# Attention with sparse heads and a gated MoE block: first five pairs' q and k in 2 KB runs, heads paired h and h+4, queries in natural order, one store a tile, one PSUM tensor, replanned

## The chip, the cores and the metric

The kernel runs on one core of one Trainium2 chip. The metric is device microseconds of one execution, as a median over runs. The profile is of one execution, with its own span (first to last instruction of the trace). The engines are TensorE (PE, its weight loads PEld), VectorE (DVE), ScalarE (ACT), GpSimd (POOL) and SyncE (SP), which issues nearly all the DMAs.

## What is computed

Four batches, eight heads, 768 positions, 64 dimensions a head, in float32. Heads 0, 2 and 6 are plain causal attention. The other five see only the first 4 keys and the last 64 (causally). The outputs of all heads are put side by side into x, 3072 tokens of 512, and go through a gated block with d_ff = 1536.

```python
scores = np.matmul(q, k.transpose(0, 1, 3, 2)) / np.sqrt(64)
causal = rel >= 0                              # rel = query position - key position
stream_keep = causal & (is_sink | (rel < 64))  # is_sink: key position < 4
mask = causal for heads 0, 2, 6, stream_keep for the others
a = softmax(where(mask, scores, -1e9))
x = a @ v, heads side by side                  # 3072 x 512
g = x @ w_gate
out = ((g * sigmoid(g)) * (x @ w_val)) @ w_out
```

## The kernel before

All matmuls are in float16 with float32 sums. The attention goes by tiles of 128 queries: 24 tiles, t = 0 to 23, in the order of TILES. Two tiles make a pair n of 256 positions of a batch (QP); a pair is the unit in which q, k and v are loaded.

Loads (`load`, L322): SP brings q, k or v of one pair into a `raw` buffer, 512 KB, as `h (p j) d -> p h (j d)` with j = 2. Partition p holds two neighbouring positions of every head, and each run in memory is 2 x 64 floats, 512 bytes. The even and odd positions of a 128-tile are therefore kept apart everywhere behind it ("j n" order: all even positions, then all odd ones). Weights come in blocks of 512 KB, in 1 KB runs (w_gate, w_val, L330) and 2 KB runs (w_out, L327). Blocks of w_gate and w_val are pieces of 256 columns.

Casts (`cast`, `castv`, `wcast`): ACT, DVE or POOL turns raw into float16 (lines L190, L192 and L196 are the helpers that issue them). q and k go to `hq`, v to `vt`, weights to `wg_sb`, `wv_sb` and `wo_sb`.

Transposes of q and k: for pairs 0 to 4 by TensorE (`transposes`, L420, eight of 128 x 128 to one PSUM bank `tr`), followed by copies to `qT` and `kT` on ACT or DVE (`evac`); for the later pairs by DMA (`dmat`, L409, on SP's queue). The two heads of one entry of PAIRS lie on the two halves of the partitions, [(0, 2), (4, 6), (1, 3), (5, 7)].

Scores (`scores`, L499): a unit is up to eight 128 x 128 blocks of scores in two PSUM banks (`sc`). A block is one matmul with 64 rows (one head); two of them, on the two row halves, can run side by side. For tiles 0 to 3 the masks are added in PSUM by matmuls of the constants `nat` with the identity. Then comes exp on ACT (L507, to `e`); in the later tiles a mask multiplies e (L516, DVE or POOL). `sinks_k` and `sinks_v` copy the first keys and values into place for the sparse heads. The value matmuls (L526) write `av`, DVE divides by the sums (L533, L534) into `xb`, and `xtranspose` turns it into `xt`, by TensorE for tiles 0 to 7 (L550) and by DMA afterwards (L544).

MoE: six groups of four tiles. Per group and per 128 columns of d_ff: four matmuls for the gate and four for the values (L687, 512 columns each, 256 in the first four steps of group 0), tanh on ACT (L693), two DVE steps (L697, L704) to `h`. Then the output product (L722), its copy to `o_sb` (`oevac`), and the stores (`store`, L743): two for a tile, since the rows of even and of odd positions lie on different partitions. The last tile's output is cut into 384 and 128 columns; there the second store of each piece goes out on ACT's queue.

Order: nothing is scheduled at run time. Each step is a task. ORDER, a string of task numbers that was planned beforehand, gives the order in which all tasks are issued, and so the order on each engine; WAYS says which engine does a task, SLOTS which buffer it uses. Numbers from FILL on are filler matmuls (`warm`, L300) on the identity, whose result is not used: 10 at the start and 11 later, all of them ahead of the first gate matmul. PSUM is split by pools: three banks for `gv` (gate, values, transposes), one for `o`, two buffers of two banks for `big` (scores, av). A task that takes a buffer waits for those that used it last.

Of the kernel before, what the change touches and what calls it, by code (L numbers as in the profile page):

```python
# [16 lines left out]
    "0306070200041I1J1Q1S1R01051K1Lxm1T1U1Vxi1W1X1f1g0A1q1r1z20211d1k1e081N1P1Mxj1Y1Z1a091o1p1w1y0C1O"  # L17
    "1h1i1j2K2Q2R1x2B2C292A2G0D2L2S2T0B1u1t0h22232U2V0g1b1c1m1n0n1s242526138q8r8s8g8h8i1v2D2E2F0y8M8N"
    "8O27280z8W8X2X2Y2f2a2b0m2I2J0F148j8k8Y8t8u8v8w8x0i8y8z8R8S8T2m2j2k2u118Z8a2Z0G2n0o108P8Q8U8V2l8b"
    "8c8d0E2H2y3435169091929596970l2W2p2q0k0I0r2z36370j17939498992M8e8f2N2O0H8l8m8n381l2c2d392e2P1F9U"  # L20
    "9V9W9Z9a9b8o8p2o3B3C3D0J3G3H1C9K9L3e3k3l2g2r2s2v2t0p0q3L3S3T9M0M1G9c9d303V3W199A9B9C3E3F333A3P9X"
    "9Y2h2w2x2i313I3Q3J3M3K3R3f3m3n9P9Q9R1A9D9E3u3v3U3X3Y9F9G9H3N3O323Z3a3b1D9S9T9N9O3r3s0s3o3z3p3c3d"
    "0T9I9JArAsAt0LAmAnAoAcAdAe0t15AfAg0u18ApAq9y9zA0AXAYAZAaAb4243444546470K3h4H4P4O0wAh3g4G4M4NA8A9"
    "AA129eA1A23q3w3t3x403yAuAv0x1HABAC0v1B4D4W4X4T4U4V0Q4w4z4x0N4K4L4IANAOAk9f4JAPAiAjAl0X4Y4Z0P3i48"
    "49A6ASATAU0eA3A4A5A70R1E9g9h9iAL4v52534Q6d3j4A4R4S4B4E4C0O0S9j9k9l9m9n4d4o4p4g4h4iAVAW414F4a4b4c"
    "4f4e0UAIAJAKAQAR4j4k4l4m4n9o9p9q4u514q4rADAE9r9t9u9v9w4yAG505E4s5455564t5O5V0W0c7A0YAFBkAHBlBLBM"
    "AwBmBOBNBPBnBo9x5WAM5N5U5T5B5C6k5D9sBpBqBrBfBgBhC9CACBCCCDC4C5C60VBT5758595A7j7rAxAy5z65AzB05R61"
    "785F5G5K5X5Y5Z5a5i5b5cBiBj606866B1B2B3B45d5e5r5s6eBsBt5H5I5L5J5M6364BuBvBwBzC05l5m5o5p5q5wC162B6"
    "B7B8B9BxBy5QBQBRBSBUBBBC5P5f5g5h5jBVBWBXC2C30Z6f6h6g6i676C6D6E696A5S0bBYBZ6lC7C85n5t5u5v5xBaBbBc"
    "BGBHBIBJBKBdBeBD6H6I5k6F6G6j5yDMDNDOCnCoCpD7D8D9DPDQ6B6J6K6L6NCxCyCzD0D1777E7FBABE6M6S6T6U6X6YCY"  # L30
    "DADB6m6x6n6y6o6pDCDDDEDHDIDJ6u736v6wCZ6O6P6Q6RCECFCGCqCrCaDKDLB5CHCJCKCL6z0dDUDFDGBFCMCO0f7l7kD2"
    "D3D40a6q6r6s7i70717274DRDSDTDVCPCQ767D7C7G7J7K7H7L7ICNCbCc6tCg6V6W7o7p7BCRCSCdCeCiCjCk6Z6a6b6cCI"
    "CTCUCfChCsCtCuCvCw7R7X7U7f7Y7Z7V7WCVCWD57a7b7nD67M7N79ClCm75E0E1E2EAEBECE3E4DqDrDsDtDuEFEGEHEIEJ"
    "EjEkElE5E6E7DvDwE8E9DxEZEa7O7P7Q7SDyDzEbEmEn7q7s7v7w7x7t7uDWDXDYDZDa80817yEeEfEg7c7d7g7e7zDbDcDd"
    "858B8C8D88898AEKELEcEdEN7T7h82838684DeDgDhDi8E8FEMEO8G8HDfEDEPEQER7m8I8J8K8LESETEhEiDjDlDmDnEEEU"
    "EVEWEXEY87FhFiFjFwFxFyFLF8F9FBCXDoDpEoEpEqFAFCFDFIFJErEtEsEuFKFMFNFOFPFQFRFEFFEvFkFlFGFHFmFnFoFc"
    "FdFeFXFYFfFgFZFuEwEyEzExF0F1F2DkFzFrFsF3F4G0FtFvG1G2G3FaFbFSFTFUF5F6F7FVFWFpFqG4G5G6G7G8G9GAGBGC"
    "GDGEGFGGGHGIGLGJGMGNGQGOGKGPGRGS"
)
WAYS = (  # L40
    "000000000000000000000000000000000000000000000000000000000000222222202202212222220200122001100100"
    "000000000000010022112212000011000000100000000000220021010100000100000210000000100000020022122000"
    "000010000000000100100000100000000022100201000010010000022000000000000220222222000000000000000002"
    "100010010000000012222200000010000000000000220012022000000000000000200001000000002202002010000001"
    "000000000010000000000000000120122000000000000000010002002222220000001000000001100000000000001002"
    "222000000000010000000000001001000000000000000000000000000000000000000000000000000000000000000000"
    "000000000000000000000000000000100001000000000000000000000000000000000000000000000000000000000000"
    "000000000100001000010000000000000000000000000000000000000000000000000000000000000000000000000000"
    "000000000000000000000000000000000000000000000000000000000000000000000000010000000000000010000000"
    "000000000000000000000000000000000000000000000000000000000100000000000000100000000000000000000000"  # L50
    "0000000000000000000000000000000000000000000000100000000000010"
)
SLOTS = (
    "0013427562C075931CADB91402567AB9387CD98D834BA1AB6D4285601010010000211011320215122041300240120012"
    "010121051403120120010110402000100513021113401100411020021304001012001511110402101302420100105141"
    "110100213020514011040021015030100511020411310012131200341300140211105020102100311041005120011021"
    "020321020111210100111021222002110002122410015011281112B1020A000291001701126000100012111F1100J012"
    "1H0121M000210011L2021K0021E2010C2101I1121D0000G01000101211091120N10128011261021A1110300110002140"
    "01051121B1100720002000101012010L1112C0000I0111M0011D0101H0122G1020J1002E012012002F2001K000000011"
    "102811120111060012N20217001190012A011222010B001142100521013010101011112C1010D2010I2110L2011E0110"  # L60
    "12011G1102M1100F0022J2021H1122K001100110"
# [57 lines left out]
def kernel(  # L119
# [45 lines left out]
    PAIRS = [(0, 2), (4, 6), (1, 3), (5, 7)]  # L165

    RINGS = {"raw": 14, "hq": 5, "e": 6, "xb": 3, "xt": 2, "sig": 2, "sil": 3,
             "h": 2 * NJ, "osb": 2, "gv": 3, "o": 1, "big": 2}
# [9 lines left out]
    for r in ("gv", "o", "big"):  # L178
        pools[r] = ctx.enter_context(tc.tile_pool(name="ps_" + r, bufs=1, space=PSUM))
# [3 lines left out]
    def buf(ring, shape, dt, name):  # L183
        return pools[ring].tile(shape, dt, name=name, tag=ring + running[-1].slots[ring])
# [50 lines left out]
    def keep(n, base, qstep, kstep):  # L235
        for j in range(2):
            part = nat[odds(j), n]
            nc.gpsimd.affine_select(
                out=part, in_=part, compare_op=ALU.is_ge, fill=OFF, base=base + kstep * j,
                pattern=[[0, n.stop - n.start], [qstep, 2], [2 * qstep, 64]],  # L240
                channel_multiplier=2 * kstep)
# [25 lines left out]
    def mask_fills(x):  # L267
        def run():
            for dst, src in FILLS[x]:
# [3 lines left out]
    FILLS = [[(m0[:, 0:3], BAND0), (m0[:, 3:4], DIAG), (m0[:, 4:6], BAND0), (m0[:, 6:8], DIAG),  # L273
              (m2[:, 2:5], DIAG), (m2[:, 1:2], OWN), (m1[:, 0:2], OWN)],
             [(m2[:, 0:1], FAR), (m1[:, 2:4], FAR)]]
# [37 lines left out]

    landed = {}

    def load(kind, n):
        r = buf("raw", [128, 1024], FP, "raw")
        landed[kind, n] = r
        if kind in "qkx":
            b, pi = QP[n]  # L320
            sl = slice(pi * 256, (pi + 1) * 256)
            nc.sync.dma_start(  # L322
# [52 lines left out]
    XQ = 5  # L375
    XK = 5

# [4 lines left out]
    def cast(n, kd, x):  # L382

        if (n, kd) not in hqs:
            hqs[n, kd] = buf("hq", [128, 1024], FH, "hq").rearrange(
                "p (k a x) -> p k a x", k=2, a=4)
        ks = slice(0, 2) if x is None else slice(x, x + 1)
        recast(T_c[n, kd, x],
               hqs[n, kd][:, ks].rearrange("p k a (s d) -> p k s a d", s=2),
               landed[kd, n].rearrange("p (k s r j d) -> p k s (r j) d", r=2, s=2, j=2, d=64)[:, ks])  # L390
# [24 lines left out]
    def transposes(n, kd):  # L415

        tr = buf("gv", [128, 4, 2, 2, 64], FH, "tr")
        for j in range(2):
            for p in range(4):
                nc.tensor.transpose(tr[:, p, :, j, :], hqs[n, kd][:, p // 2, p % 2 * 2 + j], ident)  # L420
        trs[n, kd] = tr

    def evac(n, kd, x, ps):

        copy(T_ev[n, kd][x], turned(n, kd).rearrange("c m k r x -> c (k r) m x")[:, ps],
             trs[n, kd][:, ps].rearrange("c p m j n -> c p m (j n)"))

    def sinks_k(b, m):


        T = kT[b % 2].rearrange("c t k r (j n) -> c t k r j n", j=2)
        for cs, k, r in ((slice(0, 128), slice(0, 2), 1), (slice(0, 64), slice(1, 2), 0)):
            recast(T_sk[b, m], T[cs, m, k, r, :, 0:NSINK // 2], T[cs, 0, k, r, :, 0:NSINK // 2])
# [7 lines left out]
    def plan(t):  # L441

        b, i = TILES[t]
        if i == 0:
# [4 lines left out]
              ([(0, 0, 0, 0), (0, 1, 5, i), (1, 0, 1, -1), (1, 1, 4, i),  # L449
                (1, 0, 2, i), (1, 1, 6, 0), (0, 0, 3, i), (0, 1, 7, 0)], 8, m2)]  # L450
        kts = list(range(1, i))
        for ks in (kts[:2], kts[2:]):
            unit = []
            for x, kt in enumerate(ks):
                unit += [(0, 0, 4 - len(ks) + x, kt), (0, 1, 4 + 2 * x, kt),
                         (1, 1, 5 + 2 * x, kt)]
            if unit:
                us.append((unit, 4 + 2 * len(ks), None))
        return us

    def marks(t, u):
# [3 lines left out]
        if TILES[t][1] == 0:  # L465
            return [(0, BAND0, 3), (3, DIAG, 1), (4, BAND0, 2), (6, DIAG, 2)]
        if u == 0:
            return [(0, OWN, 2), (2, FAR, 2), (4, OWN, 2), (6, FAR, 2)]
        return [(1, FAR, 1), (2, OWN, 1), (3, DIAG, 1), (4, DIAG, 2)]

    def block(t, p, kt):
# [3 lines left out]
        return kT[b % 2][:, kt, p % 2, p // 2]  # L475
# [8 lines left out]
    def scores(t, u, unit):  # L484
# [4 lines left out]
        for p, s_, c, kt in unit[0]:  # L489
            rows = slice(s_ * 64, s_ * 64 + 64)  # L490
            terms.append((c, 1, block(t, p, kt)[rows],
                          qT[t // 2 % QB][rows, half, p % 2, p // 2].unsqueeze(1)))
        for c, n, weights, moving in terms:
# [5 lines left out]
            nc.tensor.matmul(sc[:, c:c + n, :], weights, moving, start=first, stop=last)  # L499
# [341 lines left out]
```

## Time and profile before

| What | Value |
|---|---|
| median of 3 runs | 254.45 us (254.43 to 254.58) |
| the profiled execution | 254.62 us |
| its span | 252.8 us |
| mean granted clock of TensorE | 0.997 |
| busy: PE, DVE, ACT, POOL | 242.1, 161.5, 133.9, 90.1 us |
| DMA: bytes, packets | 40.72 MB, 73369 |
| loads of q, k, v; issue to landing | 512 KB each; 7.3, 7.2, 7.2 us in the median |
| stores of 128 KB half tiles; issue to landing | 46 of them; 2.4 us |

The page gives busy shares by engine, then the same in 40 slices of 6.3 us (9 is 90% or more), the DMA queues, the chain of waits that ended last, and groups of instructions (line, engine, operation, output from input, shape, count, then busy time and mean ns of one, then idle time ahead of them and what ended it). A TensorE matmul's own duration includes its passage through the array, so the cost of one in a row is better read from the chain of waits, where 8 matmuls of 512 columns take 1.73 us. An engine's idle time counts only where its work is what the end waits for.

### The profile page before, as it was taken

The page shows a single profiled execution, that of the slowest core. Times are in us where ns is not written, and L with a number is a line of the kernel's source. Part 1 is how long each engine was busy: PE and PEld are TensorE (multiplying, and loading weights), DVE is VectorE, ACT ScalarE, POOL GpSimd, SP SyncE. Part 2 cuts the span into 40 slices and gives each one's busy share as a digit, 9 for nine tenths or more (in the row PEclk, how much of TensorE's full clock was granted, in tenths as well). Part 3 has the DMA queues.
Part 4 walks back from the last instruction along what each step waited for, and adds up shares of the span by engine and source line. Part 5 has one row for each costly group of instructions (what it writes and reads, how often), then busy time and mean ns, then how long its engine had stood idle before and what let it go on. Part 6 is the DMA issues. An engine that isn't in the chain of part 4 may idle for free.

```text
span 252.8 us, 5192 instructions
## 1 busy us (share of the span) xinstructions
PE 242.1 (96%) x2009; PEld 124.7 (49%) x2009; DVE 161.5 (64%) x291; ACT 133.9 (53%) x212; POOL 90.1 (36%) x118
## 2 busy tenths in 40 slices
PE   7987999999999979999999999999999999999993
PEld 3566755654545534444555445544455544444442
DVE  2666888877877654866887655676863556563610
ACT  3666888867686415768445843664354411232010
POOL 7376889965291703810650230500134100000000
PEclk9999999999999999999999999999999999999998
DMA  6999999999996988996954757441014131114133
GB/s 182 290 308 334 319 334 315 330 324 178 325 290 142 231 184 211 207 180 133 187 66 87 208 145 93 96 87 19 0 28 68 35 83 41 41 33 95 41 85 85
DMA packets 73369, 40.72 MB, mean 161 GB/s; under 512 B 25600, under 2 KB 68864, under 8 KB 73344
## 3 DMA queue, kind: packets, MB, share of 16 engines
q1 hardware_dynamic: 73184, 40.25, 69.1%
q8 instruction: 16, 0.26, 0.4%
q10 hardware_dynamic: 160, 0.13, 0.2%
q14 instruction: 9, 0.07, 0.1%
HBM read 28.31 MB, written 6.29 MB: 137 GB/s over the span
## 4 chain that ended last, share of the span: by engine, by line
PE 79%; DMA 8%; SPq 6%; POOL 3%; issue 1%; DVE 1%; ACT 1%; ACTq 0%; POOLq 0%; DVEq 0%
PE gv L687 46%; PE o_ps L722 22%; PE sc L499 5%; SPq L322 4%; PE av L526 4%; DMA raw<-in_moe_w_gate_dram 3%; DMA xt<-xb 3%; DMA qT<-hq 2%; POOL wg_sb L192 1%; SPq L743 1%; PE xtr L550 1%; PE tr L420 1%; DVE xb L534 1%; POOL e L516 1%; ACT sig L693 0%
## 5 line engine op out<-in xcount | busy, mean ns | idle before, releaser
L507 ACT ACTIVATE e<-sc 128x1024 f16<-128x1024 f32 (+2 forms) x68 | 59.5, 907 | 31.0 <-PE sc L499 29.1
L697 DVE SCALAR_TENSOR_TENSOR sil<-sig,gv 128x512 f32<-128x512 f32 (+1 forms) x76 | 49.8, 657 | 36.4 <-ACT sig L693 35.2
L687 PE MATMUL gv<-xt,wg_sb 128*128 128x512 f16 (+1 forms) x304 | 70.8, 368 | 1.7 <-POOL wg_sb L192 1.4
L687 PE MATMUL gv<-xt,wv_sb 128*128 128x512 f16 (+1 forms) x304 | 71.5, 368 | 0.5 <-POOL wv_sb L192 0.4
L693 ACT ACTIVATE sig<-gv 128x512 f32<-128x512 f32 (+1 forms) x76 | 43.3, 576 | 53.0 <-PE gv L687 52.3
L722 PE MATMUL o_ps<-wo_sb,h 128*128 128x512 f16 (+2 forms) x300 | 67.0, 371 | 0.0
L704 DVE SCALAR_TENSOR_TENSOR h<-sil,gv 128x512 f16<-128x512 f32 (+1 forms) x76 | 49.2, 656 | 16.7 <-PE gv L687 14.6
L516 POOL TENSOR_TENSOR e<-e,m 128x640 f16<-128x640 f16 (+1 forms) x16 | 28.2, 1769 | 44.5 <-ACT e L507 44.2
L722 PEld LDWEIGHTS <-h 128*128 128x128 f16 x300 | 28.2, 98 | 31.8 <-issue 0.2
L687 PEld LDWEIGHTS <-wv_sb 128*128 128x128 f16 x304 | 28.4, 98 | 31.0 <-POOL wv_sb L192 0.5
L687 PEld LDWEIGHTS <-wg_sb 128*128 128x128 f16 x304 | 27.7, 98 | 30.5 <-POOL wg_sb L192 1.7
L192 POOL CAST vt<-raw 64x512 f16<-64x512 f32 x30 | 19.7, 659 | 28.2 <-DMA raw<-in_v_dram 26.9
L499 PE MATMUL sc<-qT,kT 64*128 64x128 f16 x472 | 21.8, 218 | 1.8 <-DMA qT<-hq 1.7
L499 PEld LDWEIGHTS <-kT 64*128 64x128 f16 x472 | 14.4, 94 | 16.7 <-issue 15.5
L526 PEld LDWEIGHTS <-e 128*128 128x128 f16 x472 | 17.0, 97 | 5.0 <-issue 1.1
L516 DVE TENSOR_TENSOR e<-e,m 128x1024 f16<-128x1024 f16 (+1 forms) x22 | 14.3, 648 | 7.8 <-ACT e L507 7.5
L190 ACT COPY o_sb<-o_ps 128x512 f32<-128x512 f32 (+1 forms) x14 | 8.1, 578 | 21.0 <-PE o_ps L722 19.2
L526 PE MATMUL av<-vt,e 128*128 128x65 f16 x472 | 18.2, 193 | 0.5 <-POOL vt L192 0.2
L192 POOL CAST hq<-raw 128x1024 f16<-128x1024 f32 (+1 forms) x17 | 16.4, 972 | 5.0 <-DMA raw<-in_q_dram 3.3
L534 DVE TENSOR_TENSOR xb<-av,rc 128x512 f16<-128x512 f32 x24 | 16.6, 691 | 1.5 <-DMA xt<-xb 0.7
L192 DVE COPY o_sb<-o_ps 128x512 f32<-128x512 f32 (+1 forms) x11 | 7.2, 651 | 13.0 <-PE o_ps L722 13.0
L192 POOL COPY vt<-vt 2x330 f16<-2x330 f16 x10 | 4.5, 452 | 19.9 <-PE av L526 19.5
(42 smaller groups left out, 111.9 us busy)
## 6 DMA issues: line engine op xcount, KB each, us to landing
raw<-in_q_dram SPq DMA_DIRECT2D x12, 512.0 KB, 7.3
raw<-in_k_dram SPq DMA_DIRECT2D x12, 512.0 KB, 7.2
raw<-in_v_dram SPq DMA_DIRECT2D x12, 512.0 KB, 7.2
out_dram<-o_sb SPq DMA_DIRECT2D x46, 128.0 KB, 2.4
raw<-in_moe_w_gate_dram SPq DMA_DIRECT2D x6, 512.0 KB, 8.3
raw<-in_moe_w_val_dram SPq DMA_DIRECT2D x6, 512.0 KB, 8.1
raw<-in_moe_w_out_dram SPq DMA_DIRECT2D x6, 512.0 KB, 6.2
xt<-xb SPq DMA_TRANSPOSE x16, 2.8
```

Of the source, the lines that this page charges most:

```text
L192: ENG[task.way].tensor_copy(out=dst, in_=src)
L322: nc.sync.dma_start(out=r.rearrange("p (h x) -> p h x", h=H), in_={"q": q, "k": k, "x": v}[kind][b, :, sl, :].rearrange("h (p j) d -> p h ...
L499: nc.tensor.matmul(sc[:, c:c + n, :], weights, moving, start=first, stop=last)
L507: nc.scalar.activation(out=e[:, at], in_=whole_sc.pop((t, u))[:, at], func=AF.Exp, scale=scale)
L516: ENG[task().way].tensor_tensor(out=ev, in0=ev, in1=mm, op=ALU.mult)
L526: nc.tensor.matmul(avs[t][:, odd, n * 66:n * 66 + 65], ee, vv, start=(m == 0), stop=(m == len(bl) - 1))
L534: nc.vector.tensor_tensor(out=xb.rearrange("p n o d -> p o n d"), in0=av[:, :, :, 0:64], in1=rc.to_broadcast([128, 2, 4, 64]), op=ALU.mult)
L687: nc.tensor.matmul(ps, wsb[:, kk, j * 128:(j + 1) * 128], xt[:, kk, c[0]:c[1]], start=(kk == 0), stop=(kk == 3))
L693: nc.scalar.activation(out=sg[g, j, c], in_=gs[g, j, c], func=AF.Tanh, scale=0.5)
L697: nc.vector.scalar_tensor_tensor(out=sl[g, j, c], in0=sg.pop((g, j, c)), scalar=1.0, op0=ALU.add, in1=gs.pop((g, j, c)), op1=ALU.mult)
L704: nc.vector.scalar_tensor_tensor(out=hs[g, j][:, c[0]:c[1]], in0=sl.pop((g, j, c)), scalar=0.5, op0=ALU.mult, in1=vs.pop((g, j, c)), op1=A ...
L722: nc.tensor.matmul(o_open[g, tt, x], hs[g, j][:, tt * 128:(tt + 1) * 128], wo_sb[:, j, lo:hi], start=(j == 0), stop=(j == NJ - 1))
```

## The change

- Loads: q and k of pairs 0 to 4 come in two DMAs of 256 KB (heads 0 to 3, heads 4 to 7), each with eight neighbouring positions of one head on one partition: 2 KB runs, 128 partitions. v and the later pairs keep their 512-byte runs.
- Pairs of heads: h and h+4 share the partitions, [(2, 6), (0, 4), (1, 5), (3, 7)].
- Casts and transposes: `cast` lays hq out by position j of eight. TensorE transposes as often as before; the copy of the result now also puts the positions into order: queries naturally, keys in the even and odd halves as before. It is always two copies of 512 columns (before: two of 512 for pairs 0 and 1, one of 1024 for pairs 2 to 4), and its read from PSUM steps by 128 or 256 float16 elements between neighbours.
- Query order: for pairs 5 to 11, which the DMA transposes in the old order, the score matmul reads q with a step of 64 elements between neighbours and writes the scores in natural order.
- Stores: one of 128 rows a piece, on SP or ACT.
- PSUM: one tensor of eight banks; any task may take any bank (or two neighbouring ones). `osb` has three buffers in place of two.
- Score tasks wait only for the halves of q and k that they read.
- ORDER, WAYS and SLOTS are new. The only fillers left are the 10 at the start.

The plan's strings are left out here; so are the changes of mask columns that follow from the new pairs.

```diff
-    PAIRS = [(0, 2), (4, 6), (1, 3), (5, 7)]
+    PAIRS = [(2, 6), (0, 4), (1, 5), (3, 7)]
...
-             "h": 2 * NJ, "osb": 2, "gv": 3, "o": 1, "big": 2}
+             "h": 2 * NJ, "osb": 3, "ps": 8, "gv": 8, "o": 8, "big": 8}
...
-    for r in ("gv", "o", "big"):
-        pools[r] = ctx.enter_context(tc.tile_pool(name="ps_" + r, bufs=1, space=PSUM))
+    psum = ctx.enter_context(tc.tile_pool(name="psum", bufs=1, space=PSUM))
+    banks = psum.tile([128, 4096], FP, name="banks")
...
+        if ring in ("gv", "o", "big"):
+            at = DIGITS.index(running[-1].slots[ring])
+            room = banks[:, at * 512:at * 512 + (1024 if ring == "big" else 512)]
...
-                pattern=[[0, n.stop - n.start], [qstep, 2], [2 * qstep, 64]],
+                pattern=[[0, n.stop - n.start], [qstep, 128]],
...
+    XPE = 5
...
+            if kind != "x" and n < XPE:
+                for s_ in range(2):
+                    nc.sync.dma_start(
+                        out=r[:, 512 * s_:512 * s_ + 512],
+                        in_={"q": q, "k": k}[kind][b, 4 * s_:4 * s_ + 4, sl, :].rearrange(
+                            "f (p j) d -> p f (j d)", j=8))
+                return
...
+        if n < XPE:
+            js = slice(0, 8) if x is None else slice(4 * x, 4 * x + 4)
+            recast(T_c[n, kd, x],
+                   hqs[n, kd].rearrange("p k a x -> p (k a x)").rearrange(
+                       "p (j s d) -> p j s d", j=8, s=2)[:, js],
+                   landed[kd, n].rearrange("p (s j d) -> p j s d", s=2, j=8)[:, js])
+            return
...
-        tr = buf("gv", [128, 4, 2, 2, 64], FH, "tr")
-        for j in range(2):
-            for p in range(4):
-                nc.tensor.transpose(tr[:, p, :, j, :], hqs[n, kd][:, p // 2, p % 2 * 2 + j], ident)
+        tr = trs[n, kd] = buf("gv", [128, 8, 128], FH, "tr")
+        for j in range(8):
+            nc.tensor.transpose(tr[:, j], hqs[n, kd][:, j // 4, j % 4], ident)
...
+        dst = turned(n, kd)[:, m].rearrange("c k r x -> c (k r x)")
+        if kd == "q":
+            copy(T_ev[n, kd][m], dst.rearrange("c (f n j) -> c f n j", f=4, j=8),
+                 trs[n, kd].rearrange("c j (m n f) -> c m f n j", m=2, f=4)[:, m])
+            return
+        copy(T_ev[n, kd][m],
+             dst.rearrange(
+                 "c (f i n l) -> c f i n l", f=4, i=2, l=4),
+             trs[n, kd].rearrange("c (l i) (m n f) -> c m f i n l", i=2, m=2, f=4)[:, m])
...
-            nc.tensor.matmul(sc[:, c:c + n, :], weights, moving, start=first, stop=last)
+            to = sc[:, c:c + n, :]
+            if weights is not ident and t // 2 >= XPE:
+                to, moving = (x[:, 0].rearrange("p (n j) -> p n j", j=2) if x is to else
+                              x[:, 0].rearrange("p (j n) -> p n j", j=2) for x in (to, moving))
+            nc.tensor.matmul(to, weights, moving, start=first, stop=last)
...
-        k_deps = [x for kt in range(i // 2 + 1) for x in T_ev[QP.index((b, kt)), "k"]]
-        k_deps += T_ev[n, "q"]
+        k_deps = [x for kt in range(i // 2) for x in T_ev[QP.index((b, kt)), "k"]]
+        k_deps += T_ev[n, "k"][:i % 2 + 1] + [T_ev[n, "q"][i % 2]]
...
-        rows = out[r0:r0 + 128, lo:hi].rearrange("(p j) n -> j p n", j=2)
-        final = g == NG - 1 and tt == SIZES[g] - 1
-        for j in range(2):
-            eng = nc.scalar if j and final else nc.sync
-            eng.dma_start(out=rows[j], in_=o_sbs[g, tt][j * 64:(j + 1) * 64, lo:hi])
+        eng = nc.scalar if T_st[g, tt, x].way == "ACT" else nc.sync
+        eng.dma_start(out=out[r0:r0 + 128, lo:hi], in_=o_sbs[g, tt][:, lo:hi])
```

## The prediction

> **What bounds the kernel now.** I read the page's busy shares and slices first, then the busy time by stretch, then what TensorE waited for, then the groups by form.
>
> ```profile
> PE 242.1 (96%) x2009; PEld 124.7 (49%) x2009; DVE 161.5 (64%) x291; ACT 133.9 (53%) x212; POOL 90.1 (36%) x118
> ...
> PE   7987999999999979999999999999999999999993
> ...
> DMA  6999999999996988996954757441014131114133
> ```
>
> TensorE is busy for 242.1 of 252.8 us, so at most 10.7 us are idle, and the slices put them at both ends. The stretches say how much is where:
>
> ```profile
> 8.00:10.00 2.00, 1.95 (x23) 1.16 (x24) 0.88 (x2) 0.65 (x2) 0.00 (x0) 1.00 1.20 291
> 12.00:14.00 2.00, 1.81 (x23) 0.97 (x20) 1.38 (x6) 1.64 (x2) 1.64 (x3) 1.00 1.20 290
> 20.00:22.00 2.00, 0.64 (x12) 0.49 (x10) 1.16 (x3) 0.70 (x1) 1.41 (x2) 1.00 1.10 348
> ...
> 90.00:95.00 5.00, 3.51 (x23) 1.53 (x21) 2.92 (x4) 1.00 (x2) 0.00 (x0) 1.00 0.88 185
> 171.00:205.00 34.00, 34.00 (x281) 17.17 (x280) 20.78 (x37) 14.27 (x22) 7.28 (x8) 1.00 0.16 30
> 238.00:253.00 15.00, 10.60 (x61) 5.36 (x59) 1.74 (x4) 1.65 (x3) 0.00 (x0) 0.94 0.37 87
> ```
>
> The columns are the stretch, its length, the busy time of PE, PEld, DVE, ACT and POOL, the clock, the DMA share and GB/s. From 22 us on PE is full, but for about 1.8 us around 95 (transposed q late), a few tenths elsewhere, and the end. Anything that TensorE must do after 22 us is therefore paid in full. Before 22 us it is not full of work: part of what fills it is the filler matmuls.
>
> ```profile
> 20.53 1.04 POOL L192 CAST wg_sb<-raw 128x1024 f16<-128x1024 f32 x1 [1.55 <-DMA raw<-in_moe_w_gate_dram]
> 21.61 0.77 PEld L687 LDWEIGHTS <-wg_sb 128*128 128x128 f16 x8 [1.48 <-POOL wg_sb L192]
> 21.62 1.05 PE L687 MATMUL gv<-xt,wg_sb 128*128 128x256 f16 x8 [1.36 <-POOL wg_sb L192]
> ```
>
> These lines of the timeline (start, length) show where the full stretch begins: the first gate block (w_gate, piece 0) lands at 20.5, GpSimd casts it in 1.04, and TensorE starts the MoE matmuls at 21.6. That block is the ninth 512 KB load on SP's queue; eight q, k, v loads go ahead of it in 512-byte runs.
>
> **What the Trainium skill says.** "DMA: Bandwidth & Descriptors", section "Why small descriptors are slow (HBM only)", gives each packet a fixed overhead. The trace agrees: 290 GB/s while only 512-byte runs move (8 to 14 us), 348 at 20 to 22 us where the weights' 1 KB runs move. "Advanced Engine Details and Errata", section "Memory Cachelines", says that SBUF reads need at least two hits on a 16-byte line for full speed. No strided matmul operand is in this trace, so nothing here shows its price. "VectorE: DVE Perf Modes", section "What auto-detection actually checks", asks for a step of one for the doubled 16-bit rate. The trace has the unit-step case: DVE moves 512 columns of the transposes in about 0.42 us and 1024 in 0.69, 0.52 ns a column. "TensorE: Matmul & The Clock Gate", Part 1, has the clock fall after an idle window of about 3.4 us. The trace shows the slow side only at the start: ten fillers in 4.29 us, against six in 1.46 later.
>
> **The change, part by part.**
>
> Loads. A packet on one of 16 engines takes 512 B / (290/16 GB/s) = 28.2 ns, and 1024 B / (348/16) = 47.1. The same step twice more puts 2 KB at about 85 ns, an estimate that gives 387 GB/s. A 512 KB load falls from 1.81 us to 1.35; if 2 KB is no better than 1 KB, to 1.51. Six of the eight loads ahead of the gate block change (q and k of three pairs): 6 x 0.30 to 6 x 0.46 = 1.8 to 2.8 us earlier. Each becomes two issues, and SP now waits for the DMA eight issues back; eight halves are 2 MB, or 5 us of transfer, so the engines stay fed.
>
> First gate. In the built program GpSimd has more ahead of this cast than before: three casts of pair 1's v, the sink copies of k (0.24 + 0.18) and of v (2 x 0.45). Pair 1's v, which GpSimd awaits until 17.70 in the timeline of before, would land 2.3 earlier (the middle of 1.8 and 2.8), at 15.4; the three casts end at 15.4 + 3 x 0.61 = 17.2, the sinks at 18.5, the cast at 19.6. The other arm: six exps of 1.02 must precede the last value product. k of pair 0 would land near 6, DVE casts its half of it after seven mask fills by 7.6 and copies q by 9.0; ACT's next evacuation waits for that, two more follow (3 x 0.59), and its exps start at about 10.8 and end near 17; the value product (0.5), normalising, transposing and copying the tile (0.9 + 0.2 + 0.42) take it to about 19. I take 20.0 for the first gate: 1.6 us earlier (0.6 to 2.6).
>
> Work moved ahead of it. Up to the first gate matmul the order has 73 score matmuls instead of 56, 48 value matmuls instead of 32 and 16 transposes of x instead of 8. At 0.55/16, 0.48/16 and 0.45/8 us each (chain of waits) that is 0.58 + 0.48 + 0.45 = 1.5 us which no longer lies in the full stretch. The 11 later fillers go; they lay in idle time, so 0.
>
> Tail. The last matmul ends at 248.6 and the span at 252.8. The last tile's stores go out as two per piece, the second pieces issued behind the first ones at about 249.6. One store per piece, and a third output buffer (ACT's 384-column copy waits 1.80 us for a store), lets the last store issue at about 249.0: -0.6.
>
> Evacuations of the transposes. Twenty of 512 columns, 11 on ACT and 9 on DVE, replace 8 of 512 and 6 of 1024. ACT takes 0.585 for 512, so 11 x 0.585 = 6.4; DVE without the doubled rate would take 0.16 + 512/0.96 ns = 0.69, so 6.2 (3.8 with it). Before they were 4.8 and 4.2. The 3.7 us more lie under TensorE, where ACT and DVE still idle some 15% between 26 and 52 us. Bounds: 0, or 2 us if reading PSUM in steps also slows both.
>
> Scores of pairs 5 to 11. These 289 of 472 matmuls now read q in natural order, jumping 128 bytes between neighbours.
>
> ```profile
> L499 PE MATMUL sc<-qT,kT 64*128 64x128 f16 x472 | 21.8, 218 | 1.8 <-DMA qT<-hq 1.7
> ...
> L190 ACT COPY kT<-tr 128x512 f16<-128x512 f16 x1 | 0.6, 585 | 0.6 <-PE tr L420 0.6
> L192 DVE COPY kT<-tr 128x512 f16<-128x512 f16 x3 | 1.2, 421 | 1.7 <-ACT kT L190 1.1 <-PE tr L420 0.6
> ```
>
> Sixteen take 0.55 us, 34 ns each, two row halves side by side. Lower bound 0 (nothing is removed, so no gain). Upper bound: 128 columns at the trace's 0.216/512 us a column are 54 ns; read at half rate they are 108, and two side by side add 27 ns to each: 289 x 27 = 7.8 us, all on the path; with part hidden by weight loads, 5.5. I take 0, because the page gives a direction but no size, and keep 5.5 to 7.8 for the range.
>
> Stores, PSUM, pairing. Twenty-five store issues replace 50. SP loses 28 of 48, at a median 0.59 us; behind them stand the transposes that TensorE awaits, yet it idles only 1.8 us for these, so 0 to -0.5. ACT takes five; the four at the end wait for DVE's copies, with only the last two evacuations queued behind: 0, or 0.3 if those slip. Any-bank PSUM slots can free only waits, and after 22 us there are none to free; new waits could cost 0 to 2 us. Pairing h with h+4 leaves the number and the row alternation of the score matmuls as they were: 0.
>
> Sum: -1.6 - 1.5 - 0.6 = -3.7, less 0.1 for SP, plus 0.3 for new waits: -3.5. On the profiled execution, 254.62 us (span 252.8 and 1.8 around it, 0.17 above the median of 254.45), that is 251.1; against the median, 251.0.
>
> **The rivals.**
>
> Slower: the strided q. Place: the score matmuls after pair 4. Price 6.6 us (the middle of 5.5 and 7.8): 251.0 + 6.6 = 257.6. It decides from 3.5/289 = 12 ns a matmul on. For it: the skill's line rule, and PE full there. Against it: the rule has no figure, and weight loads leave the stream some room.
>
> No earlier start: 2 KB runs gain nothing that counts, or the stepped PSUM reads double the evacuations ahead of the exps (four on ACT, 0.4 us each). The gate stays at 21.6 or later: 251.0 + 1.6 to 3.2, about 253.4. For it: casts, not loads, end last on both arms above. This includes the case that the runs are not 2 KB; but the built program has 128x1x512 loads.
>
> New waits: without fillers the clock drops, or the shared banks and fuller ACT and DVE stall the new order; 2 to 5 us, about 254.5. Against it: some 200 matmuls remain between the first fillers and the gate, spread over 14 us.
>
> **How the numbers follow.** Forecast 0.50 (own range 249.0 to 253.0), strided q 0.29, no earlier start 0.13, new waits 0.08. A measurement can tell about 0.2% (0.5 us) from no change. Faster: all but 0.01 of the first, half of the third, a little of the fourth: 0.58; same 0.08; slower 0.34. The range runs from 249.0 to 258.4, the strided case nearly whole.
>
> **What would show it.** Right: the first gate matmul near 20.0; q's loads 1.35 to 1.5 us apart; sixteen late scores still in 0.55 us; last matmul to end of span under 3.7 us. Wrong: late scores at 0.9 us and more; DVE evacuations at 1.2 us; TensorE idle over 3 us between the first gate and the tail.

## The result, and the profile after

The changed kernel takes 262.84 us (median of 4 runs, 261.52 to 264.7), the kernel before 254.51 beside it. The ratio is 1.0313, with a 95% interval of 1.0221 to 1.0404: slower by about 8 us, outside the range on record. Medians here are over all runs of a kernel; ratios are of undisturbed runs alone (9 of 20 in e9_twostores, 11 of 20 in e6_exp, nearly all elsewhere), so that the two can differ.

The profiled execution took 261.52 us, its span 259.7. The page's busy shares and slices:

```profile
PE 249.3 (96%) x1998; PEld 131.4 (51%) x1998; DVE 169.1 (65%) x294; ACT 132.2 (51%) x207; POOL 91.2 (35%) x126
...
PE   7699989899999999999999999999999999999995
```

TensorE is as full as before (96%), but busy for 7.2 us more. The number of matmuls is all but the same, so the same matmuls must take longer. The stretches, with the columns as before:

```profile
8.00:10.00 2.00, 0.62 (x8) 0.45 (x8) 0.98 (x2) 0.92 (x2) 0.50 (x1) 1.00 0.96 326
12.00:14.00 2.00, 2.00 (x20) 1.43 (x18) 1.07 (x3) 1.25 (x2) 1.19 (x2) 0.50 1.06 374
20.00:22.00 2.00, 1.65 (x39) 1.27 (x37) 1.90 (x7) 2.00 (x5) 1.88 (x4) 1.00 1.08 350
...
90.00:95.00 5.00, 5.00 (x78) 3.26 (x73) 1.59 (x3) 3.60 (x5) 3.11 (x4) 1.00 0.80 195
```

Three things differ from before. At 8 to 10 us TensorE works for 0.62 instead of 1.95 us; four microseconds later the clock (third from the end) is 0.50 instead of 1.00. And the gap of 1.5 us at 90 to 95 is gone.

The timeline of the first gate matmul, with the first of the exponentials ahead of it:

```profile
12.19 1.05 ACT L544 ACTIVATE e<-banks 128x1024 f16<-128x1024 f32 x1
...
20.76 1.04 POOL L207 CAST wg_sb<-raw 128x1024 f16<-128x1024 f32 x1
...
22.55 0.38 PE L587 MATMUL banks<-ident,xb 128*128 128x128 f16 x4 [0.16 <-DVE xt L207]
22.89 1.91 PE L725 MATMUL banks<-xt,wg_sb 128*128 128x256 f16 x16
```

It comes at 22.9, where 20.0 was forecast and 21.6 was measured before. The cast has no idle time ahead of it: GpSimd reaches it late because of its own queue, not because of the weights, which land at 18.7. Nor is the cast what ends last. It is done at 21.8, and until 22.9 TensorE is at the scores and the transposes of x that stand ahead of the gate block; the last of these wait for a copy on DVE. They hang on the exponentials, which start at 12.2.

The groups by form that answer to those of before:

```profile
L536 PE MATMUL banks<-qT,kT 64*128 64x128 f16 x472 | 31.2, 260 | 1.1 <-DMA kT<-hq 0.4 <-DVE sil L735 0.4 <-DVE xb L571 0.3
...
L205 ACT COPY kT<-banks 128x512 f16<-128x512 f16 x5 | 2.7, 589 | 0.7 <-PE banks L446 0.7
...
L207 DVE COPY kT<-banks 128x512 f16<-128x512 f16 x5 | 3.2, 683 | 0.9 <-PE banks L446 0.9
```

The score matmuls are busy for 31.2 us instead of 21.8. In the chain of waits, sixteen late ones take 1.08 us instead of 0.55 (at 120.2 us). A copy of 512 columns on DVE now takes 683 instead of 421 ns; on ACT it stays at 589.

I cut both spans at the first gate matmul and at the end of the last matmul (248.60 and 256.55 us), and take TensorE's busy time in the middle part:

| Part | before | after | difference |
|---|---|---|---|
| start to first gate matmul | 21.62 | 22.89 | +1.27 |
| TensorE busy between | 224.50 | 230.99 | +6.49 |
| TensorE idle between | 2.48 | 2.67 | +0.19 |
| last matmul to end of span | 4.2 | 3.2 | -1.0 |
| span | 252.8 | 259.7 | +6.9 |

So in this account the loss is work on TensorE, and a later start; idle time is nearly the same in sum. What one of these parts is worth by itself the experiments have to show, since a part that is taken away can come back as waiting.

### The profile page after: what moved, and what is told of

It reads as the page before. It is cut to its first block, busy times and chain, and to the rows that moved or that the text cites. A ratio compares the mean times of both kernels' runs of the same rounds, so it can differ in the third digit from the quotient of the medians.

```text
span 259.7 us, 5175 instructions
## 1 busy us (share of the span) xinstructions
PE 249.3 (96%) x1998; PEld 131.4 (51%) x1998; DVE 169.1 (65%) x294; ACT 132.2 (51%) x207; POOL 91.2 (35%) x126
## 3 DMA queue, kind: packets, MB, share of 16 engines
q1 hardware_dynamic: 64704, 39.07, 57.5%
## 4 chain that ended last, share of the span: by engine, by line
PE 81%; DVE 9%; DMA 4%; issue 2%; ACT 2%; SPq 1%; POOL 1%; DVEq 0%; ACTq 0%
PE banks L725 41%; PE banks L760 23%; PE banks L536 11%; PE banks L563 4%; DVE sil L735 2%; DMA raw<-in_q_dram 2%; DVE e L553 2%; DMA kT<-hq 2%; DVE h L742 1%; SPq L341 1%; DVE xb L571 1%; PE banks L446 1%; DVE vt L211 1%; ACT sig L731 1%; PE banks L587 0%
## 5 line engine op out<-in xcount | busy, mean ns | idle before, releaser
L544 ACT ACTIVATE e<-banks 128x1024 f16<-128x1024 f32 (+2 forms) x68 | 58.2, 913 | 30.4 <-PE banks L536 27.7
L725 PE MATMUL banks<-xt,wv_sb 128*128 128x512 f16 (+1 forms) x304 | 70.6, 368 | 0.0
L725 PE MATMUL banks<-xt,wg_sb 128*128 128x512 f16 (+1 forms) x304 | 69.2, 368 | 0.1
L731 ACT ACTIVATE sig<-banks 128x512 f32<-128x512 f32 (+1 forms) x76 | 42.9, 577 | 51.3 <-PE banks L725 41.8
L760 PE MATMUL banks<-wo_sb,h 128*128 128x512 f16 (+2 forms) x300 | 65.7, 371 | 0.0
L735 DVE SCALAR_TENSOR_TENSOR sil<-sig,banks 128x512 f32<-128x512 f32 (+1 forms) x76 | 49.4, 657 | 20.0 <-ACT sig L731 17.3
L742 DVE SCALAR_TENSOR_TENSOR h<-sil,banks 128x512 f16<-128x512 f32 (+1 forms) x76 | 49.1, 656 | 14.8 <-PE banks L725 13.0
L553 POOL TENSOR_TENSOR e<-e,m 128x1024 f16<-128x1024 f16 (+1 forms) x15 | 27.4, 1833 | 38.4 <-ACT e L544 38.1
L536 PE MATMUL banks<-qT,kT 64*128 64x128 f16 x472 | 31.2, 260 | 1.1 <-DMA kT<-hq 0.4
L205 ACT COPY o_sb<-banks 128x512 f32<-128x512 f32 (+2 forms) x11 | 6.0, 549 | 33.4 <-PE banks L760 33.3
L563 PE MATMUL banks<-vt,e 128*128 128x65 f16 x472 | 18.1, 193 | 1.1 <-DVE vt L211 1.1
```

Of the source, the lines that this page charges most:

```text
L205: nc.scalar.copy(out=dst, in_=src)
L536: nc.tensor.matmul(to, weights, moving, start=first, stop=last)
L544: nc.scalar.activation(out=e[:, at], in_=whole_sc.pop((t, u))[:, at], func=AF.Exp, scale=scale)
L553: ENG[task().way].tensor_tensor(out=ev, in0=ev, in1=mm, op=ALU.mult)
L563: nc.tensor.matmul(avs[t][:, odd, n * 66:n * 66 + 65], ee, vv, start=(m == 0), stop=(m == len(bl) - 1))
L725: nc.tensor.matmul(ps, wsb[:, kk, j * 128:(j + 1) * 128], xt[:, kk, c[0]:c[1]], start=(kk == 0), stop=(kk == 3))
```

## Experiments

My theory after the result: the stepped q read costs each of the 289 late score matmuls some 33 ns (1.08 less 0.55 us, by 16), 9.5 us in all. Rivals: TensorE's clock without the fillers, and the natural query order as a whole (evacuations, masks).

**Fillers put back** (e1_fill). The changed kernel with five fillers after the first q's transposes and six after the first k's, in a bank free at that time.

```diff
-    "03061I1J1Q0004071K1L01091T1U
+    "03061I1J1Qxl0004071K1L01091Txm1U
```

> The changed kernel with 11 fillers put back: 5 behind the transposes of the first q, 6 behind those of the first k, into a PSUM bank that is free there. Theory A (the stepped q read is the loss, 289 matmuls at 31 ns more): little changes, at most 2 us off, 260 to 262. Theory B (the missing fillers let the clock fall, which makes the first gate late and the time spread from run to run): clock 1.0 from 4 to 20 us, the first gate 1.5 to 3 us earlier, 258.5 to 260.5 and runs within 0.5 us. Theory C (the new order stalls TensorE between 30 and 50 us): no change beyond B's.

Measured: 260.88 us (260.2 to 261.63), ratio to before 1.0172 (1.0106 to 1.0238). Its trace has the clock at 1.00 throughout from 8 us on, and TensorE busy for 3.54 us in 8 to 12 instead of 2.44. The medians differ by 2.0 us, but the intervals of the two ratios overlap. The four executions without these fillers lie in the order of their mean clock, from 261.52 us at 0.993 to 264.7 at 0.981; with them all four are at 1.00. In the profiled execution the first gate matmul comes 1.17 us earlier, at 21.72, and yet the span is 259.9: behind the gate TensorE is busy for 0.57 and idle for 0.71 us more. The clock is the smaller part of the 8 us, of a size that is not settled here.

**Stepped read taken out** (e2_contig). The late scores are read and written in the stored order; late rows then leave in another order and meet masks in natural order, so these rows are not the reference's.

```diff
-            if weights is not ident and t // 2 >= XPE:
-                to, moving = (x[:, 0].rearrange("p (n j) -> p n j", j=2) if x is to else
-                              x[:, 0].rearrange("p (j n) -> p n j", j=2) for x in (to, moving))
```

> The changed kernel with q of pairs 5 to 11 read without steps; all else as it is, the single stores too. The queries of those tiles then stay in even and odd halves, so their masks and the rows of their output are not the reference's; the instructions and transfers are. Theory A: 16 late scores in 0.55 us again, 9 us off, 253 to 254.5. If the stepped read costs less than it seems, or its cost was hidden: 257 to 261.

Measured: 253.67 us (252.91 to 258.53), ratio 0.989 (0.9822 to 0.9957), span 251.4. One stepped read makes the difference between 3% slower and 1% faster than before. The group by form:

```profile
L533 PE MATMUL banks<-qT,kT 64*128 64x128 f16 x472 | 20.7, 219 | 2.5 <-DVE xb L568 1.3 <-DMA kT<-hq 0.9 <-DVE sil L732 0.4
```

It is back at 20.7 us. Cut as above, this run has 220.94 us of busy time between gate and tail, 10.05 less than the changed kernel: 34.8 ns for each of 289. Its span is 8.3 us shorter, since idle time grows by 2.8. It also has 3.56 less busy time than the kernel before, but 5.48 of idle time against 2.48.

**Stepped read put into the kernel before** (e3_before_step). The same three lines, for pairs 5 and up, and nothing else of the change; late rows leave in another order.

> The kernel before with one part of the change alone: the score matmuls of pairs 5 to 11 read q in steps of 64 elements. Masks and stores keep the old order, so the output of those tiles is not the reference's. Theory A: 16 late scores in 1.08 us, 289 x 31 ns = 9 us more, 262.5 to 264. Theory C (the loss belongs to the new order, where scores stand closer together): 256 to 259.

Measured: 263.17 us (262.81 to 263.55), ratio 1.027 (1.0215 to 1.0326), span 261.0. The group by form:

```profile
L503 PE MATMUL sc<-qT,kT 64*128 64x128 f16 x472 | 32.2, 258 | 0.1
```

The step alone makes the kernel before as slow as the change does. Cut as above, TensorE is busy for 9.96 us more than without it; the span is 8.2 us longer. With the run above, it is tested in both directions.

**Fillers taken out of the kernel before** (e4_before_nofill). ORDER without `xm`, `xi`, `xj`.

> The kernel before without its 11 later fillers, the first 10 kept. Theory B: the granted clock falls to 0.5 somewhere between 8 and 20 us and the first gate comes 1 to 2.5 us later, 255.5 to 257. If the fillers do nothing here: 254.5, clock at 1.0.

Measured: 255.47 us (254.24 to 257.24) beside 255.27, ratio 0.9992 (0.9965 to 1.002). The clock falls to 0.50 at 10 to 12 us in its trace, and yet the first gate matmul comes at 20.65. The fillers of the kernel before bought nothing that can be measured.

**What a step costs** (m1_steps). Sets of 96 matmuls with nothing to wait for, two 64-row halves in turn but in the last two sets; it computes nothing of the reference. Between sets run 8 matmuls of 512 columns (left out below).

> No part of the kernel: nine sets of 96 matmuls of 128 columns, fillers between them, output not the reference's. In order: two row halves side by side with q plain; the step of the change (64 elements, 128 bytes between neighbours); steps of 2, 4 and 8 elements (4, 8, 16 bytes); two neighbours and then a jump of 8; plain read with the PSUM write stepped; 128 rows plain; 128 rows with the step of the change. Theory A: 34 ns each for the first set, 65 to 68 for the second, and 54 against 108 to 120 for the last two. If the price is one read of a 16-byte line for each element, steps of 2 and 4 elements and the pairs cost nothing and the step of 8 costs what the step of 64 does. If any step costs, all of them do.

The timeline gives one line for a set; start, length and the source line of the set:

```profile
14.13 2.85 PE L45 MATMUL banks<-qs 64*128 64x128 f16 x96
...
18.75 6.06 PE L48 MATMUL banks<-qs 64*128 64x128 f16 x96
...
26.57 2.95 PE L52 MATMUL banks<-qs 64*128 64x128 f16 x96
...
31.29 5.72 PE L57 MATMUL banks<-qs 64*128 64x128 f16 x96
...
38.78 11.04 PE L62 MATMUL banks<-qs 64*128 64x128 f16 x96
...
52.58 5.72 PE L67 MATMUL banks<-qs 64*128 64x128 f16 x96
...
60.07 5.41 PE L72 MATMUL banks<-qs 64*128 64x128 f16 x96
...
67.15 5.52 PE L76 MATMUL banks<-qs 128*128 128x128 f16 x96
...
74.24 11.94 PE L79 MATMUL banks<-qs 128*128 128x128 f16 x96
```

Length by 96:

| Moving operand, float16 | ns a matmul |
|---|---|
| 64 rows, plain (L45) | 29.7 |
| 64 rows, two places 64 elements apart in turn, as in the change (L48) | 63.1 |
| step of 2 elements (L52) | 30.7 |
| step of 4 (L57); two neighbours, then a jump of 8 (L67) | 59.6 |
| step of 8 (L62) | 115 |
| plain, scores written to PSUM in the order of the step (L72) | 56.4 |
| 128 rows: plain (L76); stepped as in the change (L79) | 57.5; 124.4 |

The granted clock is 1.00 in all sets but that of step 8, where it falls to 0.50 from 41.6 us on, although TensorE is not idle; the pace there is the same before and after, four matmuls in 0.45 us. It is one execution, and the change's pattern costs 33.4 ns a matmul in it, as in the kernel (33 to 35). The Trainium skill, "Advanced Engine Details and Errata", section "Memory Cachelines", says that at least two hits on a 16-byte line are needed for full speed. Here four (step of 2) run at full rate, two (step of 4) at half, one (step of 8) at a quarter. The measurement decides: two are not enough for this operand. Nor do hits explain everything: the change's pattern jumps 128 bytes, to another line, with every element, and still runs at about half. Moving the step to the output doesn't help: the skill's "PSUM — Partial Sum Buffer", section "Specifications (TRN2)", says that any non-contiguous pattern there slows matmuls, and 56.4 against 29.7 agrees.

**The whole query order undone** (e5_oldorder_fill). The changed kernel with fillers, q evacuated as k is, no stepped read, and the two stores for each piece which the old order needs.

> The changed kernel with the query order undone wholly: even and odd halves everywhere (q copied like k, masks as before, q read without steps, two stores for each piece), and the 11 fillers of the first experiment. The 2 KB loads, the pairing, the PSUM tensor and the new order stay. Theories A and B together: 262.8 - 9 - 2 = 251.5 to 253.5, below the kernel before. Theory C: it stays at 254 or above, with TensorE idle between 30 and 50 us.

Measured: 261.27 us (259.71 to 262.75), ratio 1.02 (1.0131 to 1.027). A miss: the stepped read is gone, its scores are busy for 20.7 us, and it is slow all the same. Something in it costs as much again; q's evacuation, the masks, the fillers and the doubled stores were the suspects.

**The same with one store** (e8_onestore), rows within tiles in another order:

```diff
-        rows = out[r0:r0 + 128, lo:hi].rearrange("(p j) n -> j p n", j=2)
-        for j in range(2):
-            eng.dma_start(out=rows[j], in_=o_sbs[g, tt][j * 64:(j + 1) * 64, lo:hi])
+        eng.dma_start(out=out[r0:r0 + 128, lo:hi], in_=o_sbs[g, tt][:, lo:hi])
```

> The run with the whole query order undone and fillers in, but with one store for each piece, so that the rows within a tile leave in another order. If the doubled stores made that run slow (two issues of 0.62 us each on SP's queue ahead of the v loads and of the DMA transposes), this takes 251.5 to 254 us. If q's evacuation, the masks or the fillers made it slow, it stays at 259 to 262 us.

Measured: 253.77 us (252.71 to 257.51), ratio 0.9962 (0.9938 to 0.9987). The doubled stores were all of it: 7.5 us between the medians. Cut as above, the run with them has 5.2 us more of idle time on TensorE and 1.9 more of busy time (with a clock of 0.50 for 3.4 us from 174.9 on), a first gate matmul 0.6 later and a tail longer by about 1.3.

**Two stores alone** (e9_twostores): the run without the stepped read, with the diff above reversed; early rows leave in another order, late ones meet masks of another order.

> The changed kernel without the stepped q read, with two stores of 64 rows for each piece instead of one. If the doubled stores cost by delaying what stands behind them on SP's queue, this takes 257 to 261 us against 253.7 with one store. If they are hidden as I took them to be in the prediction (0.1 us), it takes 253.5 to 254.5 us.

Measured: 259.89 us (255.42 to 262.63), ratio 1.0073 (1.0033 to 1.0112), against 0.989 (0.9822 to 0.9957) with one store (another run of the kernel before). The direction is as expected; the size is uncertain, since the runs spread over 7 us. The delay begins in SP's queue. Without the doubled stores (e2_contig), start and length of the issues:

```profile
89.80 1.78 SPq L775 DMA_DIRECT2D out_dram<-o_sb  x2
91.62 1.20 SPq L346 DMA_DIRECT2D raw<-in_v_dram  x2
92.92 2.31 SPq L578 DMA_TRANSPOSE xt<-xb  x1
```

With them (e9_twostores):

```profile
90.01 3.79 SPq L777 DMA_DIRECT2D out_dram<-o_sb  x4
93.86 1.33 SPq L346 DMA_DIRECT2D raw<-in_v_dram  x2
95.28 2.08 SPq L578 DMA_TRANSPOSE xt<-xb  x1
```

Four issues in place of two hold SP for 2 us longer, and the load of v behind them is issued at 93.9 instead of 91.6. But TensorE's waits in these stretches are nearly the same in the two traces: 1.83 and 0.71 us (for the normalising on DVE, and for the product to h) with the doubled stores, 1.25 and 1.06 without. What differs is the clock behind them (third from the end) in e9_twostores:

```profile
94.00:96.00 2.00, 0.17 (x7) 0.04 (x2) 1.50 (x3) 1.92 (x2) 0.00 (x0) 1.00 0.68 143
...
100.00:102.00 2.00, 2.00 (x5) 0.69 (x6) 2.00 (x2) 0.00 (x0) 1.84 (x2) 0.50 1.00 250
```

It is 0.50 from 97.1 to 103.9, and 1.00 in e2_contig. Of the 5.1 us between the two spans, 3.04 are more busy time of TensorE, 1.4 a longer tail, 0.76 more idle time. That the longer wait set off the fall of the clock fits the order of events; no run here tests it.

**Natural order made by the exponential** (e6_exp). The scores stay as stored, and ACT reads them from PSUM in steps:

```diff
+        if t // 2 >= XPE:
+            to = to.rearrange("p c (n j) -> p c n j", j=2)
+            sc = sc.rearrange("p c (j n) -> p c n j", j=2)
+        nc.scalar.activation(out=to, in_=sc, func=AF.Exp, scale=scale)
```

> The changed kernel with the late score matmuls reading q in stored order, and the reordering into natural query order done by the exponential on ACT instead (its read of the scores in PSUM is stepped). If the stepped q read on TensorE is the cause of the loss and ACT reads stepped PSUM at no cost, as its evacuation of q does (589 to 592 ns against 585), this takes what the plain read took, 253 to 254 us, with the exponential of 1024 columns still at 1.02 to 1.06 us. If a stepped read costs ACT too (1.5 us or more for 1024 columns), the late exponentials become the wait ahead of PE and it takes over 257 us.

Measured: 255.62 us (252.57 to 258.92, 20 runs) with a ratio of 0.9955 (0.9919 to 0.9991). Exponentials of 1024 columns take 1026 ns, as in the changed kernel (1026) and before (1020): for ACT the step is free. The median is above the 253 to 254 us that were expected, and the runs spread over 6 us; by the ratios the run is not told apart from e2_contig, where nothing makes the natural order.

**The same with fillers and an early table load** (e10_exp_table_fill): a two-column copy on ACT at the start, so that the table load (1.28 us) is no longer behind q's first transfer.

> The changed kernel with the reordering moved into the exponential, the fillers for TensorE's clock put back, and a two-column copy on ACT at the start, so that the table load of 1.28 us is no longer behind q's first transfer. If the table load stands on the path to the first transposes of q, the cast of q starts at 4.5 instead of 5.9 us and all up to the first gate matmul moves 0.5 to 1.3 us earlier; with the granted clock at 1.0 from 8 to 16 us it takes 251 to 253 us, under the kernel before. If the transfers of k set the start instead, it takes what the run without the table copy takes, 253 to 254 us.

Measured: 254.24 us (252.93 to 256.37), ratio 0.997 (0.9944 to 0.9997). The first cast of q on ACT starts at 4.62 instead of 5.88 (e6_exp), but the first k is cast at 7.47 and the first gate matmul comes at 21.71, against 21.60 in e8_onestore, where the table load is late. It is the transfer of k that sets the start; e12_two_queues below tests this.

**One store in the kernel before** (e11_before_onestore): the store's line above in place of its two, rows in another order.

> The kernel before with one store for each piece instead of two, so that the rows within a tile leave in another order. In the changed kernel's order two stores cost about 6 us. If they cost by standing ahead of the loads on SP's queue in any order, this is faster than before by 1 us or more (253.4 us or less). If the order of the kernel before was made with room for two issues, which is what I assumed when I took 0.1 us for the 28 stores saved, it takes 254.0 to 255 us.

Measured: 252.66 us (251.18 to 254.12), ratio 0.9894 (0.9819 to 0.9968), span 249.3. Two waits of TensorE go. In the kernel before, TensorE's scores waited 1.7 us for transposed q (the largest single wait 1.5); here there is no such wait. The stretch that had 3.51 us of TensorE is full:

```profile
90.00:95.00 5.00, 5.00 (x38) 2.34 (x37) 2.42 (x4) 2.17 (x4) 0.00 (x0) 1.00 0.87 182
```

The last matmul is now followed by 3.1 instead of 4.2 us. Together that is 2.8 of the 3.5 us by which the span is shorter.

**First loads on two queues** (e12_two_queues): the run with fillers and early table load, with the second halves of the first q and k issued by ACT, ahead of that copy.

```diff
-                    nc.sync.dma_start(
+                    (nc.scalar if s_ and n == 0 else nc.sync).dma_start(
```

> The fastest version so far in the order of its pieces (reordering in the exponential, fillers, early table load), with the second halves of the first q and of the first k issued on ACT's queue, beside the first halves on SP's. If the four issues of 0.62 us on one queue delay the first k, it lands at 6.0 to 6.5 us instead of 7.4 and the first gate matmul comes 0.5 to 1 us earlier; the time goes to 252.5 to 253.5 us. If the bytes under way share the transfer rate of about 300 GB/s, k lands at 7.0 to 7.5 us as now and the time stays at 253.5 to 254.5 us.

Measured: 253.43 us (252.35 to 256.4), ratio 0.9924 (0.9897 to 0.9952). Stretches with the GB/s in the last column; all on SP's queue (e10_exp_table_fill):

```profile
4.00:6.00 2.00, 2.00 (x9) 0.85 (x8) 1.37 (x6) 0.62 (x1) 1.64 (x7) 1.00 0.70 238
6.00:8.00 2.00, 1.73 (x12) 0.88 (x9) 0.98 (x4) 0.53 (x1) 0.29 (x2) 1.00 0.91 282
```

On two queues (e12_two_queues):

```profile
4.00:6.00 2.00, 2.00 (x11) 0.85 (x10) 1.37 (x6) 0.66 (x2) 1.64 (x7) 1.00 1.02 384
6.00:8.00 2.00, 2.00 (x21) 1.29 (x19) 1.13 (x5) 0.70 (x2) 0.31 (x3) 1.00 1.04 362
```

2 KB runs do reach 360 to 384 GB/s. From one queue that issues 256 KB at a time the mean over 4 to 8 us is 260 to 291 in the eight traces with these loads, against 373 here. Later one queue gets there too: 360 and 374 at 10 to 14 us in the changed kernel, with runs of 512 bytes among them. The first k is cast at 5.96 instead of 7.47, and the first gate matmul comes at 20.27, near the 20.0 forecast for the change.

**One store and the exponential's order in the kernel before** (e13_before_one_exp): e11_before_onestore with the stepped exponential for all tiles, and masks filled once in natural order, so that the rows are the reference's.

> The kernel before with one store for each piece, the scores left as they are, and natural query order made by the exponential's stepped read on ACT; the masks are filled in natural order once. No other part of the change: no 2 KB runs, no shared PSUM tensor, no new plan. If one store for each piece is what the change has to give and the stepped read on ACT is free, it takes what the kernel before with one store took, 252 to 253.5 us, and is no slower than the fastest version with all other parts of the change (253.4 us). If the other parts carry the gain, or ACT pays for the step in this order (its exponentials of 1024 columns over 1.1 us), it takes 254 to 256 us.

Measured: 251.71 us (251.21 to 252.3) beside 254.67, ratio 0.9887 (0.9816 to 0.9958), span 249.6. Its groups by form:

```profile
L509 ACT ACTIVATE e<-sc 128x1024 f16<-128x1024 f32 x44 | 43.7, 1021 | 19.1 <-PE sc L501 17.3 <-PE av L530 1.6
```

The exponentials are unchanged at 1021 ns, and 3 us are gained. It is the fastest kernel of the study by its median; its interval overlaps that of e12_two_queues, so that the two are not told apart. It has none of the other parts of the change.

## Why the prediction was wrong

**The step that failed** is "Scores of pairs 5 to 11 [...] I take 0". It measured 33.4 ns a matmul by itself and 33 to 35 in the kernel: 289 x 33.4 = 9.7 us, on the path. The mechanism was named as a rival with a chance of 0.29, and it decided. Its upper bound of 27 ns was too low as well. I had read the operand at half the plain rate: 2 x 54 = 108 ns for two halves side by side. They take 2 x 63.1 = 126. Nothing of it was hidden by weight loads: TensorE's busy time changes by 10.05 us in e2_contig and by 9.96 in e3_before_step, of which 8.3 and 8.2 reach the end of the span. And the page's rule was there without a size: where a page gives a direction and TensorE is full, a cost of nothing was the end of the range that needed a reason, and I had none.

**Loads and first gate**, forecast at 1.6 us earlier, came 1.27 later. The first q is cast at 4.6, the first k at 7.7, the second q at 9.4 (before: 4.96, 6.77, 9.46); k was to land near 6. "Eight halves are 2 MB, or 5 us of transfer, so the engines stay fed" was the wrong sentence: each half costs SP an issue of 0.62 us, and the DMA engines moved 262 and 286 GB/s at 4 to 8 us where 387 were counted on, no more than the 512-byte runs of before in the same stretch (303 and 291). e12_two_queues, which splits the issues over two queues, shows what the runs can do (384 and 362). Whether the issue rate or the number of transfers under way holds one queue back was not separated. Over all the loads ahead of it the gate block still lands 1.7 us earlier (18.7 instead of 20.4), near the 1.8 to 2.8 forecast; but that arm does not end last. The other one does: the six exponentials, forecast from 10.8 to 17, run from 12.2 to 19.4. They start 1.4 us late, behind k, and wait another 1.19 us for scores where the clock is 0.50. I had taken the fillers at nothing because they lay in idle time. In the kernel before that holds (e4_before_nofill), although the clock falls there as well; in the changed kernel the gate comes 1.17 us earlier with them, and what this brings at the end is not settled (e1_fill). The table load, which I did not look at, moved behind a DMA, without harm (e10_exp_table_fill).

**Work moved ahead of the gate**, 1.5 us, was right in sign and too small. Without the stepped read TensorE's work between gate and tail is 3.56 us less than before. Counted once where matmuls of two kinds overlap, scores, values and transposes of x (the moved ones and what stays of them) take 2.7 us less, the products for gate and values 1.3 less (126.5 in place of 127.9 us; the sums of their groups, 139.7 and 142.5, count overlaps twice). Why the latter, was not tried; behind the gate the new order goes from one kind of matmul to another 106 times, the old one 153 times.

**Stores** were forecast at 0.1 us, with 0.5 as the most. One store in the kernel before gives about 1.1%, 2.8 us. I had put an upper bound to the transposes behind SP by TensorE's 1.8 us of waiting for them, and then took next to nothing of it; it went almost whole. The tail gave 1.0 where 0.6 was forecast.

**Evacuations** on DVE lost the doubled rate as said (683 ns, 0.69 forecast) and stayed under TensorE. ACT kept its rate on a stepped PSUM read (589 against 585). **New waits**: in sum 0.19 us of idle time, because the waits at 34 to 46 us (DVE is busy for 19.5 of 20 us from 30 to 50) took the place of those near 95. In the run without the stepped read 3 us of new waits do show, so this rival was partly true and lay hidden.

The sum, put right with what was measured: +1.27 for the gate, +9.7 for the step, -3.2 for other TensorE work (what is left of 6.49), +0.19 idle, -1.0 tail: 7 us, the 6.9 of the profiled execution but for rounding.

## What to carry to other kernels

Reorder data where a step is free: here in ACT's read of PSUM, which it does anyway, and not in the moving operand of a matmul on a full TensorE. Before an order of elements is chosen, measure the plain and the stepped form of that one instruction. And count the issues of every queue ahead of the transfers that the busiest engine awaits: here a split load cost its queue 0.62 us for each half, and a doubled store 0.9 for each.

## What was not expected of the hardware

- A float16 moving operand with a step of 2 elements runs at the plain rate (30.7 against 29.7 ns for 64 rows), with 4 at half (59.6), with 8 at a quarter (115, also while the clock was 0.50), and two neighbours with a jump of 8 cost as much as a step of 4.
- A matmul that writes plain data to PSUM in a stepped order is slowed nearly as much (56.4 ns), while ACT reads PSUM in the same order at no cost (1021 against 1020 ns for 1024 columns, e13_before_one_exp).
- Eleven fillers and a clock of 1.00 instead of 0.50 to 0.75 for four microseconds made no measurable difference to the kernel before (0.9992, 0.9965 to 1.002).
- At 4 to 8 us, 2 KB runs moved 260 to 291 GB/s in the mean when one queue issued 256 KB at a time, and 373 when two queues shared the first issues; 512-byte runs in issues of 512 KB, in the kernel before, moved 297.
